# Forgetting attention and GELU MLP: the first pair's q and k through the hardware DMA queues in fp32, and decay weights as reciprocals of a running product

## The chip, the cores and the metric

The kernel runs on one core of one Trainium2 chip. Its metric is the device time of one execution in microseconds; the time before is the median of 7 runs.

## The reference

Attention with a forget gate f in (0.8, 1), for 8 batches of 8 heads, 576 positions and head size 64, and then a two-layer MLP with exact GELU on all 4608 tokens:

```python
scores = scale * np.matmul(q, k.transpose(0, 1, 3, 2))
log_f = np.log(np.clip(f, 0.0001, 1.0))
cum = np.cumsum(log_f, axis=-1)
decay = cum[:, :, :, None] - cum[:, :, None, :]
scores = np.where(causal, -1000000000.0, scores + decay)
attn = np.exp(scores - np.max(scores, axis=-1, keepdims=True))
attn = attn / (np.sum(attn, axis=-1, keepdims=True) + 1e-09)
x = np.matmul(attn, v)                    # heads side by side: 4608 x 512
out = gelu(x @ w_in) @ w_out              # 512 -> 2048 -> 512
```

`causal` marks the keys behind the query's position. In a row of the softmax the term of the query's own position, cum[query], is a common factor and falls out. What is left is a weight for each key, exp(-cum[key]), up to one constant for each head.

## The kernel before, in words

The program is one hand-written order of instructions for each engine. It runs through the 8 batches; within a batch the heads go in 4 pairs (`HP`), and the keys of a head in 5 blocks of 128 (`NBLK`; the last block overlaps and its lower half is zeroed).

**Loads.** `load_qk_tokens` (L95) loads q and k through POOL's software DMA queue, which casts fp32 to bf16 on the way. For the first batch it is called for two heads at a time: twice at L126 and L127, then at L150 and L158, between POOL's `affine_select`s that make the identity `key_of`, the mask `after` and `ident_fp`. SP's queue loads f (L125), and then v in ten pieces (`load_v`, L114; called at L152 and L159); these wait for POOL's memset of one column of `v_sb` (L151). 

**Decay weights.** f (64 heads and batches x 576) is clipped (L185, VectorE), its logarithm is taken (L186, ScalarE), a scan adds it up into `cum` (L188, VectorE), and an exponential of the negated sum, shifted by the sum at the middle, gives `wk` (L566, ScalarE). Ln and Exp need one table load each (shown at L186 and L190, where a one-element Exp, `spark`, brings the second forward). TensorE transposes `wk` into `psw` (L576), and VectorE copies it to `wT` (L580, L581), from where it goes into the last column of the weighted v (L582).

**The first batch** is `first_attention` (L553). `warm_up(n)` (L192) issues n matmuls whose result nobody reads. `transposes_first` (L201) turns one pair's q or k tokens into qT or kT through PSUM: twelve TensorE transposes (L207) and a copy, for pair 0 on ScalarE (q, L221) or half on each of VectorE and ScalarE (k, L218 and L219), else on VectorE (L216). `scores(b, i, t)` (L279) computes one of four score tiles of pair i on TensorE (L299) into one of two PSUM buffers, and ScalarE's Exp (L309) empties it. `weigh_v` (L263, instruction at L268) multiplies v by the decay weights, for pairs 0 and 1 on VectorE, for the others on POOL. `attend` (L330) multiplies the exponentials with the weighted v; `normalize` divides (L343, L344); `to_xT` (L363, L366) transposes for the MLP. The order around the change is L564 to L618. In it pair 3's transposes stand ahead of pair 2's second score tile, and the weighing of v stands behind all of VectorE's copies for qT and kT. `gate(0, 4)` (L595) makes POOL wait until the first half of v has landed before it issues the MLP's weights (`load_w_in`).

**After that** the MLP's first GEMM of a batch (L385, GELU at L405) and the attention of the next batch follow one another on TensorE, with the second GEMM (L421, L479, L517) woven in.

Of the kernel before, what the change touches and what calls it, by code (L numbers as in the profile page):

```python
# [8 lines left out]
FP32 = mybir.dt.float32  # L9
BF16 = mybir.dt.bfloat16  # L10
Act = mybir.ActivationFunctionType
Alu = mybir.AluOpType
PSUM = bass.MemoryType.PSUM

P = 128
S = 576
D = 64
# [3 lines left out]
K0 = [0, 128, 256, 384, 448]  # L21
TC = 512

JT = 6
PT = 96
# [27 lines left out]
def kernel(  # L53
# [10 lines left out]
    nc = tc.nc  # L64
    B = q.shape[0]
    assert tuple(q.shape) == (B, H, S, D)
    BH = B * H
# [7 lines left out]
    scale = 1.0 / (D ** 0.5)  # L75
# [3 lines left out]
    consts = ctx.enter_context(tc.tile_pool(name="consts", bufs=1))  # L79
# [13 lines left out]
    qk_of = {}  # L93

    def load_qk_tokens(b, h0=0, h1=H, which="qk"):  # L95

        if b >= B:
            return
        if b not in qk_of:
            qk_of[b] = [  # L100
                qk_pool.tile([PT, H, JT * D], BF16, tag=n, name=f"{n}{b}")
                for n in "qk"
            ]
        for n, src, dst in zip("qk", (q, k), qk_of[b]):
            if n not in which:
                continue
            nc.gpsimd.dma_start(  # L107
                dst[:, h0:h1, :],
                src[b, h0:h1].rearrange("h (p j) d -> p h (j d)", j=JT),
            )  # L110

    v_sb = consts.tile([P, H, NBLK, D], FP32)

    def load_v(b, h0=0, h1=H):  # L114
        if b >= B:
            return
        for n in range(NBLK):
            p0 = D if n == NBLK - 1 else 0
            nc.sync.dma_start(
                v_sb[p0:P, h0:h1, n, :],  # L120
                v[b, h0:h1, K0[n] + p0 : K0[n] + P].rearrange("h p d -> p h d"),
            )

    f_sb = consts.tile([BH, S], FP32)
    nc.sync.dma_start(f_sb, f.rearrange("b h s -> (b h) s"))  # L125
    load_qk_tokens(0, 0, 2)  # L126
    load_qk_tokens(0, 2, 4)  # L127


# [3 lines left out]
    ident_fp = consts.tile([P, P], FP32)  # L133
# [35 lines left out]
    def load_w_in(c):  # L169
        f4 = slice(c * d_ff // 4, (c + 1) * d_ff // 4)  # L170
        nc.gpsimd.dma_start(w_in_sb[:, :, f4], w_in_r[:, :, f4])
# [4 lines left out]


    wT = consts.tile([P, NBLK, BH], FP32)
    ones = consts.tile([BH, S], FP32)
    lf = f_sb  # L180
    cum = consts.tile([BH, S], FP32)
    wk = f_sb
    nc.vector.memset(ones, 1.0)
    nc.vector.memset(wT[0:D, 4, :], 0.0)
    nc.vector.tensor_scalar(f_sb, f_sb, 1e-4, 1.0, Alu.max, Alu.min)  # L185
    nc.scalar.activation(lf, f_sb, Act.Ln)  # L186
    nc.vector.memset(v_sb[0:D, :, 4, :], 0.0)
    nc.vector.tensor_tensor_scan(cum, ones, lf, 0.0, Alu.mult, Alu.add)  # L188
    spark = consts.tile([1, 1], FP32)
    nc.scalar.activation(spark, ones[0:1, 0:1], Act.Exp)  # L190

    def warm_up(n):  # L192

        ps = m_psum.tile([P, TC], FP32, tag="m", name="ps_w")
        for _ in range(n):
            nc.tensor.matmul(ps, warm[:, 0:P], warm, start=True, stop=True)
# [4 lines left out]
    def transposes_first(b, i, which, pool, tag):  # L201

        src = qk_of[b][which]
        ps = pool.tile([P, JT, PT], BF16, tag=tag, name="ps_f")
        for j in range(JT):
            for h in range(2):
                nc.tensor.transpose(  # L207
                    ps[h * D : (h + 1) * D, j, :],
                    src[:, 2 * i + h, j * D : (j + 1) * D],
                    ident_bf[:PT, :PT],  # L210
                )

        dst = (qT, kT)[which][i].rearrange("d (p j) -> d p j", j=JT)
        src = ps.rearrange("d j p -> d p j")
        if b or i:
            nc.vector.tensor_copy(dst, src)  # L216
        elif which:
            nc.vector.tensor_copy(dst[:, 0 : PT // 2], src[:, 0 : PT // 2])  # L218
            nc.scalar.copy(dst[:, PT // 2 :], src[:, PT // 2 :])  # L219
        else:  # L220
            nc.scalar.copy(dst, src)  # L221
# [36 lines left out]
    def vw(b):  # L258
        if b not in vw_of:
            vw_of[b] = v_pool.tile([P, H, NBLK, D + 1], BF16, tag="vw", name=f"vw{b}")  # L260
        return vw_of[b]

    def weigh_v(b, i, eng=nc.gpsimd):  # L263

        hs = slice(2 * i, 2 * i + 2)
        bh = b * H + 2 * i
        w = wT[:, :, bh : bh + 2].rearrange("p n h -> p h n")
        eng.tensor_tensor(  # L268
            vw(b)[:, hs, :, 0:D],
            v_sb[:, hs, :, :],  # L270
            w.unsqueeze(3).to_broadcast([P, 2, NBLK, D]),
            Alu.mult,
        )
        if b:
            eng.tensor_copy(vw(b)[:, hs, :, D], w)
# [47 lines left out]
    def attend(b, i, h, ms):  # L323
        if (b, i, h) not in o_of:
            o_of[b, i, h] = o_psum.tile([P, NBLK, D + 1], FP32, tag="o", name="o")
        o = o_of[b, i, h]
        for m in ms:
            for n in range(m + 1):
                t, c = where(n, m)
                nc.tensor.matmul(  # L330
                    o[:, m, :],
                    e_of[b, i, t][:, h, c : c + P],
                    vw_of[b][:, 2 * i + h, n, :],
                    start=(n == 0),
                    stop=(n == m),
                )

    def normalize(b, i, h):
        if (b, i) not in x_of:
            x_of[b, i] = x_pool.tile([P, NBLK, 2, D], BF16, tag="x", name="x")  # L340
        o = o_of[b, i, h]
        r = x_pool.tile([P, NBLK], FP32, tag="r", name="r")
        nc.vector.reciprocal(r, o[:, :, D])  # L343
        nc.vector.tensor_tensor(  # L344
            x_of[b, i][:, :, h, :],
            o[:, :, 0:D],
            r.unsqueeze(2).to_broadcast([P, NBLK, D]),
            Alu.mult,
        )
# [193 lines left out]
    def gate(h, n):  # L543

        t = x_pool.tile([P, 1], FP32, tag="gate", name="gate")
        nc.gpsimd.tensor_copy(t[D:P], v_sb[D:P, h, n, 0:1])
# [6 lines left out]
    def first_attention():  # L553


        def transposes(i, pool, tag):
            transposes_first(0, i, 0, pool, tag)
            transposes_first(0, i, 1, pool, tag)

        def attend_head(i, h):  # L560
            attend(0, i, h, (0, 1, 2, 3, 4))
            normalize(0, i, h)

        warm_up(9)  # L564
        transposes(0, o_psum, "o")
        nc.scalar.activation(  # L566
            wk, cum, Act.Exp, bias=cum[:, S // 2 : S // 2 + 1], scale=-1.0
        )
        warm_up(2)
        scores(0, 0, 0)  # L570
        scores(0, 0, 1)
        transposes(1, m_psum, "m")
        scores(0, 0, 2)
        psw = o_psum.tile([P, NBLK, BH], FP32, tag="o", name="psw")
        for n in range(NBLK):
            nc.tensor.transpose(  # L576
                psw[:, n, :], wk[:, K0[n] : K0[n] + P], ident_fp[:BH, :BH]
            )
        scores(0, 0, 3)
        nc.vector.tensor_copy(wT[:, 0:4, :], psw[:, 0:4, :])  # L580
        nc.vector.tensor_copy(wT[D:P, 4, :], psw[D:P, 4, :])  # L581
        nc.vector.tensor_copy(  # L582
            vw(0)[:, :, :, D], wT[:, :, 0:H].rearrange("p n h -> p h n")
        )
        scores(0, 1, 0)
        transposes(2, m_psum, "m")
        scores(0, 1, 1)
        scores(0, 1, 2)
        scores(0, 1, 3)
        transposes_first(0, 3, 0, m_psum, "m")  # L590
        scores(0, 2, 0)
        transposes_first(0, 3, 1, m_psum, "m")
        weigh_v(0, 0, nc.vector)
        weigh_v(0, 1, nc.vector)
        gate(0, 4)  # L595
        load_w_in(0)
        load_w_in(1)
        weigh_v(0, 2)
        weigh_v(0, 3)
        load_w_in(2)  # L600
        nc.gpsimd.memset(v_sb[:, :, 0, 0:1], 0.0)
        load_v(1, 0, 4)
        load_w_in(3)
        load_qk_tokens(1, 0, 4)
        load_qk_tokens(1, 4, 8)
        load_w_out(0)
        scores(0, 2, 1)
        heads = [(i, h) for i in range(3) for h in range(2)]
        for i, t in ((2, 2), (2, 3), (3, 0), (3, 1), (3, 2), (3, 3)):
            scores(0, i, t)  # L610
            attend_head(*heads.pop(0))
        to_xT(0, 0, nc.vector.tensor_copy)
        to_xT(0, 1, nc.scalar.copy)
        attend_head(3, 0)
        both = s_psum.tile([P, 2, 1024], BF16, tag="s", name="ps_x2")
        to_xT(0, 2, nc.scalar.copy, ps=both[:, 0, 0:XC])
        attend_head(3, 1)
        gemm1_begin(0, both)  # L618
# [197 lines left out]
```

The softmax here doesn't subtract the row's maximum and nothing guards it: scores larger than these inputs give would overflow.

## Time and profile before

| | |
|---|---|
| median of 7 runs | 341.18 us (340.8 to 343.47) |
| the profiled execution's own time | 343.47 us |
| its span in the trace | 341.5 us |
| TensorE busy | 330.3 us, 97% |
| ScalarE, VectorE, POOL busy | 62%, 54%, 36% |
| mean granted clock | 0.995 |
| DMA: read from HBM, written to it | 36.85 MB, 9.44 MB |

The profiled execution is the slowest of the seven. Times in the trace are counted from the start of its span. In the lines, PE is TensorE's matmul, PEld its weight load, DVE VectorE, ACT ScalarE, SP the engine that issues loads and stores. A piece of the chain is given as start, length and name; a timeline line has start, length, engine, line, operation, output and inputs, shape and count, and in brackets the idle time before it and what ended it. In a group, the numbers behind the bar are total busy us, the mean ns of one instruction, and idle time before with its cause.

### The profile page before, as it was taken

Reading aid. Unit: us, or ns where it says so; the run is one execution under the profiler, and the core shown is the slowest. Engines: PE = TensorE matmul, PEld = TensorE weight load, DVE = VectorE, ACT = ScalarE, POOL = GpSimd, SP = SyncE. Lnnn points to the kernel's source line nnn. Section 1 sums busy time; section 2 is a strip of 40 time slices with the busy share of each in tenths; the row PEclk is TensorE's granted clock in tenths of the full one; section 3 lists DMA queues with packets and bytes.
Section 4 is the critical chain, followed back from the end, with each engine's and each line's share of the span. In section 5 each row is a group of like instructions: output and inputs, shape, how many; then the busy total and the mean of one; then the engine's idle time right before and its main releaser. Section 6 shows DMA issues by size and latency. Waiting matters only on the chain.

```text
span 341.5 us, 7835 instructions
## 1 busy us (share of the span) xinstructions
PE 330.3 (97%) x3170; PEld 172.2 (50%) x3170; DVE 184.2 (54%) x417; ACT 210.1 (62%) x299; POOL 122.0 (36%) x250
## 2 busy tenths in 40 slices
PE   7699989999999999999999999999999999999995
PEld 3484555444554456545654565445544654444443
DVE  5661265853556945796479646974596641020011
ACT  6867697673553787378737973787468755504600
POOL 8190367038335134533455242724351420000000
PEclk9989999999999999999999999999999999999999
DMA  8999999979998989497968598589910241011013
GB/s 112 184 158 190 207 191 148 187 114 185 157 203 198 140 168 198 117 138 98 213 170 119 99 219 154 98 136 192 180 45 2 68 86 50 0 62 63 0 36 89
DMA packets 104628, 44.18 MB, mean 129 GB/s; under 512 B 83408, under 2 KB 100048, under 8 KB 104592
## 3 DMA queue, kind: packets, MB, share of 16 engines
q1 hardware_dynamic: 87296, 29.52, 46.3%
q0 software_dynamic: 16896, 13.63, 26.9%
q8 instruction: 25, 0.41, 0.5%
q10 hardware_dynamic: 400, 0.52, 0.4%
q14 instruction: 11, 0.09, 0.1%
HBM read 36.85 MB, written 9.44 MB: 136 GB/s over the span
## 4 chain that ended last, share of the span: by engine, by line
PE 91%; DMA 2%; POOL 2%; ACT 2%; issue 1%; DVE 1%; POOLq 0%; DVEq 0%; ACTq 0%
PE ps L385 36%; PE ps L479 27%; PE o L330 9%; PE ps L421 8%; PE s L299 7%; DMA k<-in_k_dram 2%; PE ps L517 2%; ACT e L309 2%; POOL q L107 1%; PE ps_x L363 1%; PE ps_f L207 1%; POOL k L107 0%; DVE vw L268 0%; DVE qT L216 0%; DVE kT L216 0%
## 5 line engine op out<-in xcount | busy, mean ns | idle before, releaser
L405 ACT ACTIVATE g<-ps 128x512 bf16<-128x512 f32 x144 | 82.1, 601 | 80.3 <-PE ps L385 80.3
L309 ACT ACTIVATE e<-s 128x896 bf16<-128x896 f32 (+2 forms) x128 | 101.0, 834 | 29.1 <-PE s L299 26.1
L385 PE MATMUL ps<-xT,w_in_sb 128*128 128x512 bf16 x512 | 112.5, 379 | 0.0
L479 PE MATMUL ps<-w_out_sb,g 64*128 64x512 bf16 (+1 forms) x736 | 108.5, 377 | 0.0
L385 PEld LDWEIGHTS <-w_in_sb 128*128 128x128 bf16 x576 | 55.9, 98 | 67.5 <-issue 1.8
L311 POOL TENSOR_SCALAR_AFFINE_SELECT e<-e 128x256 bf16<-128x256 bf16 (+1 forms) x135 | 49.2, 383 | 95.9 <-ACT e L309 95.6
L479 PEld LDWEIGHTS <-g 64*128 64x128 bf16 (+1 forms) x736 | 41.9, 94 | 39.8 <-issue 9.0
L299 PE MATMUL s<-qT,kT 64*128 64x320 bf16 (+4 forms) x384 | 45.8, 278 | 3.0 <-ACT e L309 1.7
L268 POOL TENSOR_TENSOR vw<-v_sb,wT 128x640 bf16<-128x640 f32 x30 | 38.8, 1294 | 22.5 <-DMA v_sb<-in_v_dram 14.0
L249 DVE COPY kT<-tk 64x288 bf16<-64x288 bf16 x96 | 44.7, 466 | 2.3 <-DMA tk<-k 0.8
L487 DVE COPY ot<-ps 128x512 f32<-128x512 f32 x25 | 17.3, 692 | 42.0 <-PE ps L479 42.0
L249 DVE COPY qT<-tq 64x288 bf16<-64x288 bf16 x96 | 38.0, 396 | 1.4
L330 PEld LDWEIGHTS <-e 128*128 128x128 bf16 x960 | 34.7, 99 | 7.4 <-POOL e L311 2.5
L330 PE MATMUL o<-vw,e 128*128 128x65 bf16 x960 | 37.4, 195 | 1.0 <-DVE vw L268 1.0
L344 DVE TENSOR_TENSOR x<-o,r 128x320 bf16<-128x320 f32 x64 | 31.5, 492 | 2.2
L430 DVE COPY ot<-ps 128x512 f32<-128x512 f32 (+2 forms) x9 | 5.7, 633 | 48.9 <-PE ps L421 48.9
L299 PEld LDWEIGHTS <-kT 64*128 64x128 bf16 x384 | 19.6, 94 | 23.7 <-issue 10.9
L421 PE MATMUL ps<-w_out_sb,g 128*128 128x512 bf16 (+2 forms) x144 | 28.0, 355 | 0.0
L343 DVE RECIPROCAL r<-o 128x5 f32<-128x5 f32 x64 | 12.1, 190 | 24.2 <-PE o L330 24.0
L421 PEld LDWEIGHTS <-g 128*128 128x128 bf16 x144 | 13.5, 98 | 14.5
L490 DVE TENSOR_TENSOR ot<-ot,ps 128x512 f32<-128x512 f32 x25 | 17.2, 688 | 1.4
L385 PE MATMUL ps<-tails,w_in_sb 128*128 128x512 bf16 x64 | 14.4, 378 | 0.0
(67 smaller groups left out, 133.3 us busy)
## 6 DMA issues: line engine op xcount, KB each, us to landing
out_dram<-ot SPq DMA_DIRECT2D x32, 256.0 KB, 2.7
v_sb<-in_v_dram SPq DMA_DIRECT2D x24, 256.0 KB, 5.1
q<-in_q_dram POOLq DMA_DIRECT2D x6, 576.0 KB, 6.1
k<-in_k_dram POOLq DMA_DIRECT2D x6, 576.0 KB, 8.1
v_sb<-in_v_dram SPq DMA_DIRECT2D x22, 128.0 KB, 4.9
w_in_sb<-in_moe_w_in_dram POOLq DMA_DIRECT2D x4, 512.0 KB, 8.3
w_out_sb<-in_moe_w_out_dram POOLq DMA_DIRECT2D x4, 512.0 KB, 8.8
q<-in_q_dram POOLq DMA_DIRECT2D x4, 144.0 KB, 4.5
```

The costliest lines, as they stand in the source:

```text
L249: nc.vector.tensor_copy(rows[:, odd], src[odd * D : (odd + 1) * D, 2 * i + h].rearrange("d j p -> d p j"),)
L268: eng.tensor_tensor(vw(b)[:, hs, :, 0:D], v_sb[:, hs, :, :], w.unsqueeze(3).to_broadcast([P, 2, NBLK, D]), Alu.mult,)
L299: nc.tensor.matmul(to, *ab, start=half < 0, stop=half == 1 or not masked)
L309: nc.scalar.activation(et[:, :, z:c], st[:, :, z:c], Act.Exp, scale=scale)
L311: nc.gpsimd.affine_select(out=et[:, :, c0 + z : c0 + P], in_=et[:, :, c0 + z : c0 + P], compare_op=Alu.is_ge, fill=0.0, base=z, pattern=[[ ...
L330: nc.tensor.matmul(o[:, m, :], e_of[b, i, t][:, h, c : c + P], vw_of[b][:, 2 * i + h, n, :], start=(n == 0), stop=(n == m),)
L344: nc.vector.tensor_tensor(x_of[b, i][:, :, h, :], o[:, :, 0:D], r.unsqueeze(2).to_broadcast([P, NBLK, D]), Alu.mult,)
L385: nc.tensor.matmul(ps, w_in_sb[:, kt, ffb * P : (ffb + 1) * P], src[:, kt, 0:TC], start=(kt == 0), stop=(kt == n_dm - 1),)
L405: nc.scalar.activation(g_of[c][ffb], ps, Act.Gelu)
L421: nc.tensor.matmul(pss[ts][:, c0:c1], g_of[c][kt][:, ts * P : (ts + 1) * P], w_out_sb[:, kt, c0:c1], start=(kt == 0), stop=(kt == n_ff - 1),)
L479: nc.tensor.matmul(banks[r], g_of[c][kt][rows, ts * P : (ts + 1) * P], w_out_sb[rows, kt, :], start=kt == (steps.index("r") if r else 0), ...
L487: nc.vector.tensor_copy(ot, banks[1])
```

## The change

The first pair's q and k (heads 0 and 1 of batch 0) leave POOL's queue. They are loaded as fp32 into two tiles of their own, q by SP's queue ahead of f, k by ScalarE's queue, and are cast to bf16 on chip, q by VectorE and k by ScalarE. The decay weights come without logarithm and exponential: one scan multiplies the clipped f up from a start of 2^80 (`decay`), and the copies of its transpose out of PSUM become reciprocals. The scan's place moves behind the first pair's transposes. `warm_up` runs 7 and 1 times instead of 9 and 2.

```diff
     f_sb = consts.tile([BH, S], FP32)
+    pair_fp = [consts.tile([PT, 2, JT * D], FP32, name=f"{n}_fp") for n in "qk"]
+    for queue, src, dst in zip((nc.sync, nc.scalar), (q, k), pair_fp):
+        queue.dma_start(dst, src[0, 0:2].rearrange("h (p j) d -> p h (j d)", j=JT))
     nc.sync.dma_start(f_sb, f.rearrange("b h s -> (b h) s"))
-    load_qk_tokens(0, 0, 2)
     load_qk_tokens(0, 2, 4)
...
-    ones = consts.tile([BH, S], FP32)
-    lf = f_sb
-    cum = consts.tile([BH, S], FP32)
-    wk = f_sb
-    nc.vector.memset(ones, 1.0)
+    none = consts.tile([BH, S], FP32)
+    decay = consts.tile([BH, S], FP32)
+    nc.vector.memset(none, 0.0)
     nc.vector.memset(wT[0:D, 4, :], 0.0)
+    nc.vector.memset(v_sb[0:D, :, 4, :], 0.0)
+    spark = consts.tile([1, 1], FP32)
+    nc.scalar.activation(spark, none[0:1, 0:1], Act.Exp)
+    nc.vector.tensor_copy(qk_of[0][0][:, 0:2, :], pair_fp[0])
+    nc.scalar.copy(qk_of[0][1][:, 0:2, :], pair_fp[1])
     nc.vector.tensor_scalar(f_sb, f_sb, 1e-4, 1.0, Alu.max, Alu.min)
-    nc.scalar.activation(lf, f_sb, Act.Ln)
-    nc.vector.memset(v_sb[0:D, :, 4, :], 0.0)
-    nc.vector.tensor_tensor_scan(cum, ones, lf, 0.0, Alu.mult, Alu.add)
-    spark = consts.tile([1, 1], FP32)
-    nc.scalar.activation(spark, ones[0:1, 0:1], Act.Exp)
...
-        warm_up(9)
+        warm_up(7)
         transposes(0, o_psum, "o")
-        nc.scalar.activation(
-            wk, cum, Act.Exp, bias=cum[:, S // 2 : S // 2 + 1], scale=-1.0
-        )
-        warm_up(2)
+        nc.vector.tensor_tensor_scan(decay, f_sb, none, 2.0**80, Alu.mult, Alu.add)
+        warm_up(1)
...
-                psw[:, n, :], wk[:, K0[n] : K0[n] + P], ident_fp[:BH, :BH]
+                psw[:, n, :], decay[:, K0[n] : K0[n] + P], ident_fp[:BH, :BH]
...
-        nc.vector.tensor_copy(wT[:, 0:4, :], psw[:, 0:4, :])
-        nc.vector.tensor_copy(wT[D:P, 4, :], psw[D:P, 4, :])
+        nc.vector.reciprocal(wT[:, 0:4, :], psw[:, 0:4, :])
+        nc.vector.reciprocal(wT[D:P, 4, :], psw[D:P, 4, :])
```

## The prediction

> **What bounds the kernel now.** I read the chain of work that ended last first, because it says which stage an edit in the start can move at all. Of its span 91% is TensorE, and after 27 us TensorE hardly rests: its idle times from there on are few and 0.83 us at most. So the change, which touches only the first 17 us, is worth what it moves the first attention, and everything behind shifts with it. The first 40 us of that chain (start, length, what):
>
> ```profile
> 7.66 7.49 DMA k<-in_k_dram
> ...
> 15.19 0.47 PE ps_f L207 x12
> ...
> 16.35 0.83 DVE vw L268
> ...
> 17.23 0.67 PE o L330 x15
> ...
> 26.93 12.18 PE ps L385 x56
> ```
>
> The reader is to see that the start is not held by the first pair: the last load of k (heads 6 and 7, issued by POOL at 7.66) lands at 15.15; then come its transposes, its copy on VectorE (L216), the weighing of v (L268) and at 17.23 the first product with v (L330). The second view is the table by stretches (length, then busy us of PE, PEld, DVE, ACT, POOL, then clock, DMA share, GB/s):
>
> ```profile
> 4.00:5.00 1.00, 0.79 (x6) 0.16 (x5) 0.79 (x2) 0.98 (x2) 0.91 (x3) 1.00 1.28 182
> 12.00:14.00 2.00, 1.41 (x35) 1.01 (x29) 1.19 (x2) 1.97 (x4) 0.00 (x0) 1.00 1.23 249
> 14.00:15.00 1.00, 0.00 (x0) 0.00 (x0) 0.05 (x1) 0.78 (x1) 0.00 (x0) 1.00 1.05 217
> 16.00:17.00 1.00, 0.21 (x6) 0.16 (x3) 1.00 (x2) 1.00 (x2) 0.98 (x2) 1.00 0.30 66
> 18.00:20.00 2.00, 2.00 (x33) 1.59 (x29) 1.17 (x4) 0.70 (x1) 2.00 (x2) 0.50 1.06 172
> ```
>
> From 4 to 15 us the 16 DMA engines are full (share 1.05 to 1.3; packets overlap), so the loads come at the rate of the engines. TensorE idles in 14 to 17, and then runs at half clock; the trace's clock record has this from 17.69 to 21.10. The third view is the timeline, TensorE and then ScalarE:
>
> ```profile
> 4.94 0.45 PE L207 MATMUL ps_f<-key_of,q 96*64 96x96 bf16 x12 [0.21 <-DMA q<-in_q_dram]
> 5.71 0.45 PE L207 MATMUL ps_f<-key_of,k 96*64 96x96 bf16 x12 [0.32 <-DMA k<-in_k_dram]
> ...
> 13.29 0.28 PE L299 MATMUL s<-qT,kT 64*128 64x256 bf16 x2
> ```
>
> ```profile
> 7.66 7.12 ACT L309 ACTIVATE e<-s 128x896 bf16<-128x896 f32 x9
> 15.98 1.62 ACT L309 ACTIVATE e<-s 128x768 bf16<-128x768 f32 x2 [1.20 <-PE s L299]
> ```
>
> Nine exponentials run without a gap from 7.66 to 14.78: until pair 2's first scores at 13.29, ScalarE paces the start. Were the last k there earlier, TensorE could take it only after these scores, at about 13.8. Last, VectorE's groups by shape up to 20 us:
>
> ```profile
> L188 DVE TENSOR_TENSOR_SCAN cum<-ones,f_sb 64x576 f32<-64x576 f32 x1 | 1.3, 1349 | 0.2 <-ACT f_sb L186 0.2
> L185 DVE TENSOR_SCALAR f_sb<-f_sb 64x576 f32<-64x576 f32 x1 | 0.5, 452 | 1.1 <-DMA f_sb<-in_f_dram 1.1
> L580 DVE COPY wT<-psw 128x256 f32<-128x256 f32 x1 | 0.4, 416 | 0.0
> L343 DVE RECIPROCAL r<-o 128x5 f32<-128x5 f32 x2 | 0.4, 196 | 0.8 <-PE o L330 0.8
> L581 DVE COPY wT<-psw 64x64 f32<-64x64 f32 x1 | 0.2, 227 | 0.0
> ```
>
> **What the Trainium skill says.** "DMA: Bandwidth & Descriptors", section "Issuing engines are not separate DMA queues": loads issued by SP, ACT and POOL run on the same 16 engines, and another issuer saves issue time only. The shares of 1.2 and more agree: the change can start loading sooner, not load faster. "TensorE: Matmul & The Clock Gate", Part 1: a window of 3413 ns with little work brings half clock. The trace agrees: 3.41 us at 0.50 after a window in which TensorE idled 1.37 and 1.01 us. "VectorE: DVE Perf Modes", in its walkthrough of the eight-slice pipeline: the reciprocal is an iterative divide with a repeat count of 8. The trace hints at it: the copies of 64 and 256 elements from PSUM (227 and 416 ns) give 164 + 0.98 ns for each element, so 169 for five; the reciprocal of five takes 196, which is 6.4 ns for each.
>
> **Part by part. First pair.** SP issues q (192 runs of 1536 bytes) at 0.81, where f stood; ACT issues k at the same time. f's packets began 1.4 us after its issue and it landed 2.6 us after; the packet records show about 58 packets started per 0.25 us when full, so the 384 packets of the pair need 1.65 us from 2.2, and more once POOL's heads 2 and 3 join at 3.0: done at about 4.15, landed at 4.5 to 4.7. The casts: VectorE, 768 elements at two per cycle (the price of fp32 from SBUF in the same VectorE page's perf-mode tier table; L185's 452 ns for 576 fits it), 0.55 us, or 0.95 at one per cycle. ScalarE: 186 + 0.833 ns x 768 = 0.83 us ("ScalarE: Activation LUTs", What ACT_TABLE_LOAD costs; that gives 666 for L186's 576, measured 683). So q's transposes start at 5.1 to 5.5 (now 4.94), k's at 5.5 (now 5.71). ScalarE's copies of qT and half of kT (612 and 399 ns) follow; the scores start at 6.4 instead of 6.71. f, now second on SP's queue, lands at about 5.0; its clip (0.45) is done before the half of kT on VectorE is due at 5.95. Below zero: if the pair lands at 4.0, 0.5 better.
>
> **Decay.** Gone from ScalarE: L186 (683), one table load (1283) and L566 (777). Only L566 was on the path: it ended at 7.76, and the first exponential began at 7.66. It now waits for its scores alone: 7.0, so 0.65 us earlier. The scan (1349) moves behind kT's half: 6.4 to 7.75, in an idle time that was 1.44 us long (6.66 to 8.10); behind it stands pair 1's qT, ready at 7.7, so it costs nothing unless the scores come later. The two reciprocals replace copies of 643 ns together. At one cycle the same 643; at 6.4 ns each 164 + 1638 + 164 + 410 = 2376; at eight cycles 2.99 us. I take 2.38, so 1.73 added. Queued behind them on VectorE: vw's column, then pair 2's qT and kT, then pair 2's first scores on TensorE. Starting at 9.25 they end at 11.6, the column at 11.9, the copies at 13.35; scores of pair 2 at 13.35 to 13.8, against 12.65 if the reciprocal were cheap. It eats ScalarE's 0.65.
>
> **Loads.** POOL drops two issues (0.81 + 0.64) ahead of all else, so heads 2 to 7, the memset of v and SP's loads of v behind it move up by 1.15 to 1.45 us. The engines start full work some 0.6 us earlier and carry the same packets. Last k: the landing record has 15 of 16 engines' increments by 13.71 and one at 15.15; on that engine a 16 KB instruction packet of 962 ns started at 13.07. Moved by 1.35 the fifteen come at 12.35; a packet of the same kind comes at about 12.3 to 13, which may or may not hit. v's first five pieces: 14.22 without the late engine, so 12.9 to 14.1. All of this is then before the scores of pair 2 end, and VectorE is what is late next.
>
> **Warm-up.** Three matmuls of 0.31 to 0.385 fewer; they filled waiting, so nothing, except for the clock (below).
>
> **Sum.** Last k's transposes 13.8, its copy 14.25 to 15.0, weighing to 15.8, first product at 15.8 instead of 17.23: 1.43 us. TensorE's idle time before it falls from 2.38 to some 1.6 us, so I let the half clock go: between 17.23 and 25.66 the chain's pieces make 7.05 us at the full-clock durations instead of 8.43, so 1.38. Profiled execution: 343.47 (span 341.48 and 1.99 around it) - 1.43 - 1.38 = 340.66. But this execution lies 2.29 above the median of the runs, which therefore lacks most likely the half clock and perhaps part of the late landing. From the median: 341.18 - 1.43 = 339.75 if the landing is late there too; if it came at 13.8, the product would start at 15.85 already and 341.1 stays. Between them, and near the profiled sum: 340.5.
>
> **Rivals.** Full gain (20%): the reciprocal takes a cycle per element; scores of pair 2 end at 13.1, first product at 15.1, 2.13 us gained. 339.05 from the median, 339.96 from the profiled sum: 339.4. For it: the 27 ns above the copies' line might be the stride of the operand. Against: that difference and the page. Absorbed (22%): median runs never had the late landing; ScalarE and VectorE pace the start before and after: 341.1. For it: the 2.29 us between profile and median. Slower (12%): the clock. With 7 warm-up matmuls TensorE is done at 4.0 and waits a microsecond for the cast; from 4.0 to 7.4 it then does some 1.9 us of work, 0.9 of it transposes. If that window counts as idle, the next 3.41 us run at half clock, with 2.9 us of work where TensorE idled only 0.5: 1.7 us lost at most, about 1.5 behind the absorbed case: 342.6. It decides where the clock falls to 0.50 between 7 and 11 us. That the path isn't touched at all I leave inside "absorbed".
>
> **How the numbers follow.** Forecast 340.5 with 46% (339.6 to 341.0). The range, 338.9 to 341.9, leaves out the slower case and the lowest end of the full gain. About 0.5% (1.7 us: below 339.47, above 342.89) is what a measurement of this kernel can tell from no change. Faster: most of the full gain and the forecast's lower edge, 0.24; slower: half of the clock case, 0.07; same 0.69.
>
> **What would show it.** Right: first exponential near 7.0, two RECIPROCALs of about 1.8 and 0.57 us, pair 2's scores waiting for VectorE's kT, last k landed before 14, first product near 15.8, no half clock around 18. Wrong: q's or k's transposes later than 5.9 (the two hardware queues get less than I give them), clock 0.50 between 7 and 11 us, v landing after the last kT, or a wait for weights of the first GEMM at 25 us.

## The result, and the profile after

The changed kernel takes 345.75 us (median of 13 runs, 343.63 to 347.74) against 341.64 us (34 runs of the kernel before, 340.63 to 344.62). The ratio is 1.0112, 95% interval 1.0086 to 1.0138: slower by 1.1%, outside the forecast's range. The profiled execution took 344.19 us with a span of 342.4 us.

The chain of work that ended last, for the kernel after (start, length, what):

```profile
0.81 4.87 DMA k_fp<-in_k_dram
5.71 0.84 ACT k L189
...
11.19 1.76 DVE wT L578
12.96 0.57 DVE wT L579
13.84 0.76 DVE qT L216
14.60 0.68 DVE kT L216
15.32 0.54 PE s L299 x12
...
16.95 1.20 DVE vw L268
18.20 0.90 PE o L330 x15
```

The last load of k is gone from the chain; it lands at 12.52. In its place stand the first pair's load of k with its cast on ScalarE, and then VectorE: two reciprocals, the copies of pair 2's qT and kT, the weighing of v. The first product with v starts at 18.20 us, where it was 17.23. The table by stretches of the kernel after:

```profile
4.00:5.00 1.00, 0.42 (x1) 0.00 (x0) 0.00 (x0) 0.00 (x0) 1.00 (x4) 1.00 1.14 224
14.00:15.00 1.00, 0.74 (x18) 0.63 (x17) 1.00 (x2) 1.00 (x2) 1.00 (x2) 1.00 0.27 37
18.00:20.00 2.00, 1.80 (x29) 1.45 (x29) 2.00 (x3) 0.65 (x2) 2.00 (x2) 0.58 1.24 205
```

In 4 to 5 us TensorE now works 0.42 us of 1.00 (0.79 before), and VectorE and ScalarE stand still: nothing of the first pair is there. In 14 to 15 the order is turned round. The DMA engines are nearly free (0.27), VectorE is full, and TensorE works. At 18 to 20 TensorE runs at about half clock again. The timeline of TensorE, and ScalarE's first exponential, both of the kernel after:

```profile
1.26 3.17 PE L196 MATMUL ps_w<-warm 128*128 128x512 bf16 x7 [1.26 <-DVE warm L137]
6.05 0.45 PE L207 MATMUL ps_f<-key_of,q 96*64 96x96 bf16 x12 [1.63 <-DVE q L188]
...
15.32 0.28 PE L299 MATMUL s<-qT,kT 64*128 64x256 bf16 x2 [0.22 <-DVE kT L216]
```

```profile
8.54 1.62 ACT L309 ACTIVATE e<-s 128x896 bf16<-128x896 f32 x2 [0.57 <-PE s L299]
```

The warm-up ends at 4.43 and TensorE then waits 1.63 us for VectorE's cast of q. The exponentials begin at 8.54 instead of 7.66, and pair 2's scores at 15.32 instead of 13.29. The clock record has 0.50 from 8.10 to 11.51 and from 18.34 to 21.75. VectorE's groups by shape up to 20 us, of the kernel after:

```profile
L268 DVE TENSOR_TENSOR vw<-v_sb,wT 128x640 bf16<-128x640 f32 x2 | 3.0, 1543 | 0.0
L578 DVE RECIPROCAL wT<-psw 128x256 f32<-128x256 f32 x1 | 1.8, 1758 | 0.2 <-PE psw L574 0.2
L566 DVE TENSOR_TENSOR_SCAN decay<-f_sb,none 64x576 f32<-64x576 f32 x1 | 1.3, 1339 | 0.0
...
L579 DVE RECIPROCAL wT<-psw 64x64 f32<-64x64 f32 x1 | 0.6, 560 | 0.0
```

The reciprocals take 1758 and 560 ns in place of 416 and 227. The weighing of v on VectorE takes 1543 ns in the mean; it took 820 before. Behind the start the two traces agree: in the 314.4 us from 26.6 (before) and 27.6 us (after) on, TensorE is busy for 308.94 and 309.01 us. So the loss lies in the first attention. In this pair of traces it is only 1.0 us, since the traced execution of the kernel before is the slowest of its seven, 343.47 us, with half clock of its own from 17.69 to 21.10; the 4.1 us between the medians have to be found in further executions.

### The profile page after: what moved, and what is told of

Read it like the earlier page. It is cut to its first block, busy times and chain, and to the rows that moved or that the text cites. A ratio compares the mean times of both kernels' runs of the same rounds, so it can differ in the third digit from the quotient of the medians.

```text
span 342.4 us, 7829 instructions
## 1 busy us (share of the span) xinstructions
PE 331.1 (97%) x3167; PEld 172.8 (50%) x3167; DVE 188.6 (55%) x418; ACT 208.7 (61%) x297; POOL 121.7 (36%) x248
## 4 chain that ended last, share of the span: by engine, by line
PE 92%; DVE 3%; ACT 2%; DMA 1%; issue 1%; DVEq 0%; ACTq 0%
PE ps L385 36%; PE ps L479 27%; PE o L330 9%; PE ps L421 8%; PE s L299 8%; PE ps L517 2%; DMA k_fp<-in_k_dram 1%; ACT e L309 1%; PE ps_f L207 1%; PE ps_x L363 1%; DVE wT L578 1%; DVE qT L216 0%; DVE kT L216 0%; DVE vw L268 0%; ACT k L189 0%
## 5 line engine op out<-in xcount | busy, mean ns | idle before, releaser
L299 PE MATMUL s<-qT,kT 64*128 64x320 bf16 (+4 forms) x384 | 47.0, 282 | 3.1 <-ACT e L309 1.9
L249 DVE COPY kT<-tk 64x288 bf16<-64x288 bf16 x96 | 42.5, 442 | 1.6
L249 DVE COPY qT<-tq 64x288 bf16<-64x288 bf16 x96 | 41.0, 428 | 1.4
L490 DVE TENSOR_TENSOR ot<-ot,ps 128x512 f32<-128x512 f32 x25 | 17.2, 687 | 1.7 <-PE o L330 0.5
```

The costliest lines, as they stand in the source:

```text
L249: nc.vector.tensor_copy(rows[:, odd], src[odd * D : (odd + 1) * D, 2 * i + h].rearrange("d j p -> d p j"),)
L299: nc.tensor.matmul(to, *ab, start=half < 0, stop=half == 1 or not masked)
```

## The experiments

Two theories stand against each other. Theory A: the start itself is slower. The first pair lands about a microsecond late, the reciprocals hold VectorE 1.7 us longer, and TensorE falls to half clock. Theory B: the loads that moved forward collide later with other traffic or work. Each ratio is to the kernel before, measured in the same session, with its 95% interval. "Microseconds" between two kernels are differences of their medians, in places across sessions.

**The changed kernel again**, no edit.

> The changed kernel once more, on a chip of its own with the kernel before beside it. Theory A (the time is lost in the first 18 us, by three things that add up: the first pair is ready about 1 us later, the two reciprocals hold VectorE 1.7 us longer, and the clock falls to half from 8 to 11.5 us): 344 to 347 us, ratio about 1.01 again, and in the trace the first product with v at 18 us or later. Theory B (the start costs little, the moved loads collide with something later): the same time, but with the first product at about 17 us and idle time of TensorE after 27 us that the kernel before does not have.

Measured: 346.17 us (344.31 to 348.11), 1.0124 [1.0087, 1.0162]. In its trace the transposes take 281 ns each instead of 206 from the first on, so TensorE was not warm in the start. "Warm" stands here for full clock. The clock record begins only at 19.18, with full clock, and the first product stands at 19.72. The loss is there again, and the clock differs from one execution to the next.

**The decay part alone**: POOL loads the first pair again, 9 and 2 warm-ups; scan and reciprocals stay.

```diff
-    pair_fp = [consts.tile([PT, 2, JT * D], FP32, name=f"{n}_fp") for n in "qk"]
-    for queue, src, dst in zip((nc.sync, nc.scalar), (q, k), pair_fp):
-        queue.dma_start(dst, src[0, 0:2].rearrange("h (p j) d -> p h (j d)", j=JT))
...
+    load_qk_tokens(0, 0, 2)
...
-    nc.vector.tensor_copy(qk_of[0][0][:, 0:2, :], pair_fp[0])
-    nc.scalar.copy(qk_of[0][1][:, 0:2, :], pair_fp[1])
...
-        warm_up(7)
+        warm_up(9)
...
-        warm_up(1)
+        warm_up(2)
```

> Only the decay part: scan of f and reciprocals as in the changed kernel, but all loads by POOL and 9 and 2 warm-up matmuls as before. Theory A: the late pair and the early half clock are gone, the reciprocals stay, with the first exponential at about 7.0 us: first product at 16 to 17.2 us, time within 1 us of the kernel before (ratio 0.998 to 1.003). Theory B (loads are the cause, decay harmless): the same or a little better than before, so this run alone does not tell A from B, but it tells both from the case that the reciprocals alone make the loss, which would give a ratio of 1.006 or more.

Measured: 341.76 us (340.63 to 345.52), 1.0015 [0.9994, 1.0035]. The first exponential is at 7.57. So the new way to the weights costs next to nothing as a whole; the loss sits in the first pair's new loads and what hangs on them. This trace, of an execution of 343.6 us, has half clock from 15.37 to 22.19 too, though the pair's transposes followed the warm-up without a wait: half clock behind 15 us is not the changed kernel's alone.

**The changed kernel without reciprocals**: copies in their place, so the weights are the products themselves, not their inverses.

```diff
-        nc.vector.reciprocal(wT[:, 0:4, :], psw[:, 0:4, :])
-        nc.vector.reciprocal(wT[D:P, 4, :], psw[D:P, 4, :])
+        nc.vector.tensor_copy(wT[:, 0:4, :], psw[:, 0:4, :])
+        nc.vector.tensor_copy(wT[D:P, 4, :], psw[D:P, 4, :])
```

> The changed kernel with plain copies in place of the two reciprocals, so the weights are the running products themselves and not their reciprocals. Theory A: VectorE is free 1.7 us earlier, pair 2's scores start 1 to 1.7 us earlier, first product near 17 us or before: 1.0 to 1.7 us under the changed kernel (ratio to before 1.005 to 1.008). Theory B: no change against the changed kernel, since the reciprocals are covered.

Measured: 344.34 us (342.22 to 347.59), 1.0071 [1.0043, 1.0099]. Its interval overlaps that of the kernel as changed, so this run alone doesn't size the reciprocals. It does show that they aren't the main part: most of the loss stays. In its trace the first product came at 18.24, not near 17 as expected, with half clock from 7.75 to 11.17 and from 17.99 to 21.41.

**More warm-up**: 12 and 2 matmuls that nobody reads instead of 7 and 1, to fill the wait for the pair.

```diff
-        warm_up(7)
+        warm_up(12)
...
-        warm_up(1)
+        warm_up(2)
```

> The changed kernel with 12 and 2 warm-up matmuls instead of 7 and 1, which fill TensorE's wait for the first pair. Theory A: the clock stays at 1.0 from 8 to 11.5 us, the first exponentials no longer wait for TensorE, and the start gains 0.5 to 1.5 us against the changed kernel (ratio to before 1.006 to 1.009). Theory B: nothing, or a loss of the added matmuls' time.

Measured: 342.76 us (341.8 to 346.8), 1.0033 [1.0009, 1.0056], against 1.0124 [1.0087, 1.0162] for the changed kernel in the same session: 3.4 us come back for six idle matmuls, where 0.5 to 1.5 were expected. The start of TensorE's timeline of this kernel:

```profile
1.26 4.05 PE L196 MATMUL ps_w<-warm 128*128 128x512 bf16 x12 [1.26 <-DVE warm L137]
6.06 0.45 PE L207 MATMUL ps_f<-key_of,q 96*64 96x96 bf16 x12 [0.75 <-DVE q L188]
```

The pair's transposes start at the same moment (6.06 against 6.05), so nothing arrives earlier; only the wait before them falls from 1.63 to 0.75 us. The table by stretches of this kernel (length, then busy us of PE, PEld, DVE, ACT, POOL, then clock, DMA share, GB/s):

```profile
7.00:11.00 4.00, 3.32 (x67) 2.23 (x68) 3.81 (x6) 3.25 (x6) 0.37 (x1) 1.00 1.30 232
...
19.00:25.00 6.00, 5.68 (x127) 4.72 (x127) 5.03 (x16) 4.87 (x7) 5.73 (x9) 1.00 1.09 171
```

The clock is 1.00 from 3.90 us to the end of the kernel's work, and the first product starts at 16.87. With the changed kernel's own warm-up, two more executions were traced, no edit:

> One more look at the changed kernel, for the state of the clock in another execution. If the spread of its times (343.6 to 348.1) is the clock's, an execution near 346 shows half clock, or matmuls of twice the length, for longer than one near 344: through most of the first 20 us and past it.

> The same as the look before, once more: half clock in the first 20 us for longer where the time is longer.

Measured: 347.78 and 346.7 us. The first has half clock from 7.86 to 11.27 and from 18.10 to 24.93, first product at 18.67. The second has it without a break from 7.36 to 24.43, first product at 19.94. The same stretches of the second:

```profile
7.00:11.00 4.00, 3.76 (x60) 2.68 (x59) 3.14 (x4) 2.50 (x5) 0.36 (x1) 0.55 1.30 235
...
19.00:25.00 6.00, 5.06 (x84) 4.03 (x83) 3.69 (x8) 2.81 (x5) 4.87 (x9) 0.55 1.16 190
```

From 19 to 25 us the records show 84 matmuls here and 127 with the warm clock, though TensorE is busy most of the time in both; from 7 to 11 it is even busier (3.76 us against 3.32) for fewer matmuls (60 against 67). It is slow, not starved. The mean clock that is listed for each run points the same way, in part. Four of the changed kernel's first 14 executions list 0.975 or 0.98; a mean of 0.975 over 344 us is 2 x 0.025 x 344 = 17.2 us at half clock, just the 17.07 us of this trace. Of 50 runs of the kernel before in the first session none is below 0.99 (in the two later ones 3 of 75 and 1 of 19). But the list leaves out what lies ahead of the record's beginning. The traced execution of 344.31 us, whose record begins at 19.18, lists 1.000, and of the first 14 those of 346.38, 347.04 and 347.67 us list 0.998 or 1.000.

The clock records of all traces say where the fall comes from. They change in steps of 3.41 us, so the stretches in which the clock is set, windows from here on, can be laid out from each record's beginning. The first window at full clock, which holds the wait for the pair, of the kernel after and then of the one with 12 and 2 warm-ups:

```profile
4.68:8.10 3.42, 1.66 (x33) 1.01 (x35) 2.23 (x4) 1.87 (x3) 2.69 (x8) 1.00 1.29 204
3.90:7.31 3.41, 2.65 (x33) 1.18 (x31) 1.52 (x3) 1.47 (x2) 3.41 (x11) 1.00 1.24 212
```

TensorE is busy for 1.66 us of the first, and half clock follows; in the second it is busy for 2.65, and full clock stays. In the other three traces with 7 and 1 warm-ups behind the late pair whose record begins in time it is 1.45 to 1.52 us, and half clock follows each time; in the other three with 12 and 2 it is 2.54 to 3.31, and full clock stays each time. All windows of the 14 traces up to 330 us sort in this way: the 11 at full clock with 2.24 us or less of busy time were followed by half clock, all the others, from 2.25 us on, by full clock. Behind 330 us four windows with 1.4 to 2.0 us kept the clock, so busy time as counted here is not the whole rule. The windows also lie differently in each execution: in 11 traces the record begins between 3.90 and 5.54 us, in the other three at 10.06, 10.58 and 19.18. That would explain why executions of one kernel are of several kinds.

**The old warm-up in the changed kernel**: 9 and 2.

```diff
-        warm_up(7)
+        warm_up(9)
...
-        warm_up(1)
+        warm_up(2)
```

> The changed kernel with the kernel before's 9 and 2 warm-up matmuls. TensorE is then done at about 4.6 us and waits 1.4 us for the first pair, against nearly no wait with 12. If what counts is how full the window of the clock's monitor is, this lies between the changed kernel (346.2) and the run with 12 and 2 (342.8), with runs of both kinds: 343.5 to 345.5. If the kernel before's number is enough, 342.8.

Measured: 344.88 us (341.94 to 346.39), 1.0095 [1.0057, 1.0133]. TensorE's timeline of this kernel:

```profile
6.39 0.69 PE L207 MATMUL ps_f<-key_of,q 96*64 96x96 bf16 x12 [1.11 <-DVE q L188]
```

The wait is 1.11 us, and the twelve transposes take 0.69 us where a warm clock gives 0.45; the clock record begins at 10.58. Half clock follows again from 17.40 to 24.23. The interval overlaps that of the changed kernel: the old number does not repair it.

**The shorter warm-up in the kernel before**: 7 and 1.

```diff
-        warm_up(9)
+        warm_up(7)
...
-        warm_up(2)
+        warm_up(1)
```

> The kernel before with 7 and 1 warm-up matmuls instead of 9 and 2, nothing else. If the number of warm-up matmuls alone makes the loss, ratio 1.006 to 1.011. If it takes the longer wait of the changed kernel too (1.63 us there; here TensorE would wait about 0.5 us for q and 0.3 for k), within 0.3% of the kernel before.

Measured: 341.93 us (340.76 to 348.43), 1.0007 [0.9989, 1.0026]. TensorE's timeline of this kernel:

```profile
5.06 0.69 PE L207 MATMUL ps_f<-key_of,q 96*64 96x96 bf16 x12 [0.63 <-DMA q<-in_q_dram]
```

So the three removed matmuls cost nothing by themselves. Here too the transposes ran at half clock, and the record begins only at 10.06, but the first product came at 16.86 all the same: with POOL's loads half clock up to 10 us need not cost anything. With one trace for each kernel, the four order by the wait between warm-up and pair: 0.63 and 0.75 us leave the time near that of before, 1.11 and 1.63 give 1.0095 and 1.0112. It is the wait for the late pair that makes the loss, not the removal of three matmuls as such.

**The reciprocals under a warm clock**: the kernel with 12 and 2 warm-ups, once with copies in place of the reciprocals (the edit shown above; the weights are again not inverted):

> 12 and 2 warm-up matmuls as in the run before, and plain copies in place of the reciprocals (the weights are then the products themselves). If VectorE's extra 1.68 us is on the path once the clock is warm, the first product comes at about 15.4 instead of 16.9 us and the time falls by 1.0 to 1.7 us to 341.1 to 341.8, the level of the kernel before. If the clock was everything, it stays at 342.8.

Measured: 342.0 us (341.56 to 346.32), 1.0006 [0.9986, 1.0027], with the first product at 16.48 where 15.4 was expected. And once with only the first batch's 8 columns inverted in the start, the other 56 copied aside and inverted in the first GEMM:

```diff
+    later = consts.tile([P, NBLK, BH - H], FP32)
...
-        nc.vector.reciprocal(wT[:, 0:4, :], psw[:, 0:4, :])
-        nc.vector.reciprocal(wT[D:P, 4, :], psw[D:P, 4, :])
+        nc.vector.reciprocal(wT[:, 0:4, 0:H], psw[:, 0:4, 0:H])
+        nc.vector.reciprocal(wT[D:P, 4, 0:H], psw[D:P, 4, 0:H])
+        nc.vector.tensor_copy(later[:, 0:4, :], psw[:, 0:4, H:])
+        nc.vector.tensor_copy(later[D:P, 4, :], psw[D:P, 4, H:])
...
+                if ffb == 6:
+                    nc.vector.reciprocal(wT[:, 0:4, H:], later[:, 0:4, :])
+                    nc.vector.reciprocal(wT[D:P, 4, H:], later[D:P, 4, :])
```

> 12 and 2 warm-up matmuls, and of the reciprocals only the 8 columns of the first batch at the old place (32 + 8 elements, about 0.6 us), the other 56 columns copied out (0.65 us) and inverted during the first GEMM, where VectorE is idle. VectorE's theory: about 1.07 us less ahead of pair 2's copies, time 341.7 to 342.2. If the clock was everything: 342.8.

Measured: 342.05 us (341.46 to 344.31), 1.0023 [1.0009, 1.0037]. Both medians lie 0.7 to 0.8 us under the 342.76 of the kernel with all reciprocals in the start. The four short instructions take 348, 210, 393 and 220 ns. The intervals of these kernels overlap; that two different edits give the same size is what supports it. The ratios scatter more than the medians: by them the two edits are worth 0.9 and 0.3 us.

**The same split without the moved loads**: the edit above on the decay part alone.

> The decay part alone with the loads of the kernel before, and the reciprocals split as in the run with the split above. Decay alone was level with the kernel before; if VectorE's reciprocals took what the shorter ScalarE chain gave, this gains 0.3 to 1 us: ratio 0.997 to 0.999. If the last loads of q and k set the time there, no change: 1.000.

Measured: 341.06 us (340.22 to 345.49), 0.9981 [0.9964, 0.9998]. That is 0.70 us under the decay part alone, a third sight of the same size by the medians (by the ratios 1.2 us, with intervals that just overlap), and the fastest version of all: 0.2% under the kernel before. It differs from the warm split kernel by the moved loads alone (and one kernel's three extra warm-ups, which fill a wait), and the intervals of the two don't overlap: the moved loads cost 0.99 us even with the longer warm-up. Its first product starts at 16.15.

**POOL's weighing held back**: in the warm split kernel POOL reads one element of VectorE's last weighed v before it weighs its own.

```diff
         load_w_in(1)
+        g = x_pool.tile([P, 1], FP32, tag="gate", name="gate")
+        nc.gpsimd.tensor_copy(g, vw(0)[:, 3, 0, 0:1])
         weigh_v(0, 2)
```

> As the run with 12 and 2 warm-up matmuls and split reciprocals (342.05), and POOL's weighing of v for pairs 2 and 3 waits until VectorE has weighed pairs 0 and 1 (one element of its result is read first). If the 1.0 us that the moved loads cost comes from POOL and VectorE weighing at the same time (819 ns grow to 1500 and 1900), VectorE's two take 820 ns each and the time falls to 341.0 to 341.6. If it comes from the first pair's later arrival, it stays at 342 or rises by POOL's delay.

Measured: 341.76 us (341.22 to 343.34), 1.0004 [0.9982, 1.0026]. VectorE's group of this kernel:

```profile
L269 DVE TENSOR_TENSOR vw<-v_sb,wT 128x640 bf16<-128x640 f32 x2 | 1.6, 822 | 0.0
```

Without this edit the two took 1493 and 1896 ns. So the long weighing is POOL's doing: shown by the trace. Its worth, 0.3 us by medians, is only indicated, as the intervals overlap.

Theory A stands in the main: the loss lies in the start. Theory B falls as far as it was looked for: behind the start TensorE idles for 5.2 to 5.5 us in four traces alike, of the kernel before, of the kernel after, of its execution of 346.7 us and of the kernel with 12 and 2 warm-ups, and the one collision found, POOL's with VectorE's weighing, lies at 16 to 20 us. By medians the steps from the kernel before to the changed one are: decay without the wait for reciprocals -0.5, moved loads +1.0, reciprocals in the start +0.7, the clock +3.4, together 4.6 us. These four are one chain of kernels, so their sum has to come near the whole difference (346.17 - 341.48 = 4.7 us) and is no check of the parts. Of the parts, the clock's and the moved loads' are between kernels whose intervals lie apart; the reciprocals' is only indicated.

## Why the prediction was wrong

**The failed step: "they filled waiting, so nothing, except for the clock".** What was put aside as an exception was the result. The removed matmuls as such are indeed worth next to nothing: the kernel before does without them (1.0007), and putting them back leaves most of the loss (1.0095). What failed is that the sum priced TensorE's wait for the pair at nothing and left the clock out. The rival that named it had 12%, and a price of one window between 7 and 11 us, 1.7 us at most. The wait from 4.4 us on set it off much as that rival said (its 1.9 us of work in that window lie under the 2.25 found above), but the half clock did not end with one window. The traces with 7 and 1 or 9 and 2 warm-ups behind the late pair show it from the first transposes on, or at 8 to 11 us and again at 18 to 25, or right through from 7 to 24, and the warm clock is worth 3.4 us by the medians. The sum went further astray with "so I let the half clock go", which booked 1.38 us of gain in the very stretch where the clock fell again. The forecast had left some 1.6 us of idle time there; in the kernel after, 1.43 us of idle time in the window from 14.92 to 18.34 were enough. This second fall follows waits ahead of the first product, as in the kernel before, so it isn't the late pair's alone; how the 3.4 us divide between the earlier and the later stretches of half clock stays open.

**The mis-sized term: "landed at 4.5 to 4.7".** q landed at 5.34 and k at 5.68. I took the packet rate of a moment when the engines are full. The records show that the packets began at 1.86 (q) and 2.14 us (k), no later than the forecast's 2.2, but only 95 or so started between 2 and 3 us, where 58 in each quarter had been taken. POOL, which issued its loads from 1.38 on, got its first packets only after 4 us, so they don't explain the slow rate, and why it was slow stays open. The casts were right in size (632 ns, forecast 550 to 950, and 832 ns, forecast 830). So q's transposes came at 6.05 instead of 5.1 to 5.5, beyond the 5.9 that the prediction itself named as a sign of error, the scores at 7.59 instead of 6.4, and the first exponential at 8.54 instead of 7.0.

**Right: the reciprocals.** 2.32 us together, forecast 2.38. (1758 - 164) / 256 and (560 - 164) / 64 both give 6.2 ns for each element. VectorE's kT of pair 2 was what came late next, as said. Right too: the last k lands before 14 (12.52), the scan isn't on the chain, and nothing behind the start moves against the rest.

**A gain that wasn't there: "so 0.65 us earlier".** ScalarE's last exponential for the weights (L566) was taken to hold up the first exponential of the scores. With the decay part alone and POOL's loads it begins at 7.57 and, with split reciprocals, at 7.60, instead of 7.66, and waits for the scores both times. In the timeline of the kernel before, the matmuls of the first score tile end at 7.48, so even there L566 held it up by less than 0.2 us. That the reciprocals then cost some 0.7 us by the medians, near what "It eats ScalarE's 0.65" says, looks like chance.

**Not foreseen: what the earlier v sets off.** v's fifth piece lands at 13.01, so POOL's gate opens early and POOL weighs its share from 16.18 on, just when VectorE weighs its own. The Trainium skill, "SBUF — State Buffer", section "Who interferes with whom", says that VectorE and GpSimd share a pair of ports and that the one who comes second is blocked for the other's whole instruction. The trace agrees in size: VectorE's first weighing starts at 16.95, while POOL's (16.18, 1281 ns) runs; it ends at 18.14, and POOL's second takes 1847 ns instead of the 1280 of the run in which POOL is held back. The weighing ended at 15.8 in the forecast, on VectorE's time alone.

**The rest of the moved loads' 1.0 us** goes with the pair's arrival: the first exponential is at 8.47 in the split kernel with POOL held back and at 7.60 in the split kernel with POOL's loads. No run changed the arrival alone, so this share is read from the traces and not isolated.

**The clock rule.** The Trainium skill, "TensorE: Matmul & The Clock Gate", section "Why this matters for your kernels", advises against idle gaps of more than about 3 us. Here less was too much: windows with 1.17 to 1.96 us of idle time, in one or more pieces, were followed by half clock. That the stretches are whole windows agrees with its Part 1: 17.07 and 6.83 us are five and two times 3.41. Up to 330 us of these traces the boundary for keeping full clock lies at about 2.25 us of busy time in a window of 3.41. What brings full clock back can't be read from them in the same way: in the longest stretch of half clock, windows with 2.26 to 3.36 us of busy time were followed by half clock again, while 2.64 us of warm-up matmuls in one window brought full clock at 3.90 us in the kernel with 12 and 2.

## What to carry to other kernels

When a change shortens a warm-up or lets the first real operands come later, treat the wait between them as a price in clock, and look at several executions: one trace of the start can show two windows of half clock, the next one five. What to compare is TensorE's busy time within the window that holds the wait, not the length of one gap. A load that moves to another queue at twice the bytes is not forecast from the packet rate of a busy moment: bound its landing from the slowest row that the trace has from issue to landing, and see what the slow end sets off. When a transfer comes earlier, follow it to the engine that it lets go, and see what that engine then runs beside.

## What the runs showed of the hardware

The loads on POOL's queue did not interleave with the hardware queues' packets at first: issued from 1.38 us on, none started before 4.04, while the pair's 384 packets ran from 1.86 to about 4.7. In the kernel before, POOL's first packets came at 2.96 after an issue at 1.39. Whether they waited for the pair or were themselves late is not shown. A load of f that was first on SP's queue took 2.6 us from issue to landing; behind q of twice the bytes it took 5.1:

```profile
q_fp<-in_q_dram SPq DMA_DIRECT2D x1, 288.0 KB, 4.5
k_fp<-in_k_dram ACTq DMA_DIRECT2D x1, 288.0 KB, 4.9
f_sb<-in_f_dram SPq DMA_DIRECT2D x1, 144.0 KB, 5.1
```

These are the DMA issues of the kernel after, up to 7 us, with the median us from issue to landing in the last column. And half clock, once there, can hold on while TensorE is busy: 17.07 us in one trace, with TensorE working 3.76 of the 4.00 us from 7 to 11.
